# 105 idle matmuls of 256 and 512 columns behind the last product of a channel attention with an ELU feed-forward

## The chip, the cores and the metric

The kernel runs on one core of a Trainium2 chip. The metric is device time in microseconds (us). Before the change three runs took 2182.03, 2182.52 and 2183.09 us; the median, 2182.52 us, is the time before. One further execution was taken with the hardware profiler on. All views quoted below are of that execution, and its own time stands beside its span.

The engines are called by the profile's names: PE is TensorE's matmuls and PEld its weight loads, DVE is VectorE, ACT is ScalarE, POOL is GpSimd, SP is SyncE. L398 is line 398 of the kernel.

## The reference

Four batches of 6080 tokens with 256 channels. Attention is over channels: the Gram matrix of the normalised q and k is taken over all tokens of a batch, its softmax is applied to v, and the result goes through a feed-forward layer with ELU.

```python
B, N, C = (4, 6080, 256)
qn = q / (np.linalg.norm(q, axis=1, keepdims=True) + 1e-06)
kn = k / (np.linalg.norm(k, axis=1, keepdims=True) + 1e-06)
s = kn.transpose(0, 2, 1) @ qn / tau
a = softmax(s)                        # over the last axis
x = (v @ a).reshape(B * N, C)
h = x @ w_in                          # 256 -> 2048
g = np.where(h > 0, h, np.exp(np.minimum(h, 0)) - 1)
out = g @ w_out                       # 2048 -> 256
```

## The kernel before

**Tiles.** Tokens are cut into chunks of 512 or 496 columns (12 to a batch, 48 in all), the 2048 hidden channels into 16 blocks of 128 (`FT`), the 256 channels into two blocks of 128 (`KT`, `DT`). Per batch the attention matrix is multiplied into `w_in` first, and gives that batch's weights `wps[b]`. The main loop then runs over the steps (chunk, hidden block): six matmuls for the hidden block (`h_item`, L360 to L362), the ELU on ScalarE and VectorE (`elu`), a split of the result in a high and a low part (`split_g`, L107 and L108), and three steps later six matmuls into the chunk's two output banks (`out_item`, L398, L400, L402; one bank for each output half). Every wide matmul streams one chunk, 512 or 496 columns, through a weight tile of 128 columns. Each matmul has a weight load of its own, and the trace shows it as PEld.

**High and low parts.** Operands are float32 split into a part that one pass of TensorE takes and the rest. So three matmuls stand for one product. `in_turns` only sets in which order the columns of a chunk are streamed.

**Narrow matmuls before.** While a batch's main loop runs, the next batch's Gram matrix is made in between: `gram_item` gives a matmul of 512 columns (L191) and one of 256 (L198) in turn, and `out_item` takes one of them after each of its own. So a matmul of 256 columns always has one of 512 ahead of it and behind it. The norms of a batch (`norms`, L218) are eight float32 matmul passes of a single column each, in a row.

**The end.** For the last chunk `store` copies the first output half on ScalarE (L425), and the second half in two quarters of the output, one on VectorE (L419) and one on ScalarE (L420); each part is sent out as soon as it is copied (L427, L421, L422). Nothing else is left then.

**Order and buffers.** TensorE works in the order of its queue. PSUM has eight banks: two for the Gram matrices, three under the tag `w` (`WB = 3`: hidden blocks, attention, norms) and three under the tag `o` (`8 - KT - WB`: outputs). A tile that takes a bank waits for the last reader, and where there is none for the last writer, of the tile that had it three tiles before. `wo` holds `w_out` in its two parts for the whole run; `wps[3]` are the last batch's weights.

Of the kernel before, what the change touches and what calls it, by code (L numbers as in the profile page):

```python
# [7 lines left out]
F32 = mybir.dt.float32  # L8
# [19 lines left out]
def in_turns(cols):  # L28

    if len(cols.shape) == 3:  # L30
        return cols.rearrange("p x (a b) -> p x b a", a=2)
    return cols.rearrange("p (a b) -> p b a", a=2)
# [691 lines left out]
                fn()  # L724


# [1 line left out]
_INS = ["q", "k", "v", "tau", "moe_w_in", "moe_w_out"]  # L728
_OUTS = [((256, 24320), "float32")]
# [26 lines left out]
```

## Time and profile before

| what | value |
|---|---|
| runs before, us | 2182.03, 2182.52, 2183.09 |
| profiled execution, us | 2182.71 |
| its span in the trace, us | 2180.9 |
| matmuls in the trace | 10232 |
| matmuls of 256 columns at L198 | 276 |
| DMA | 118.15 MB, mean 54 GB/s |

The span is the time from the first to the last instruction of the trace; 1.81 us of the profiled execution lie around it. Busy time of an engine is the sum of its instructions' records. Matmul records overlap, since one begins while the one ahead is still draining, so their spacing from start to start is what a matmul costs in a stream. A timeline row has the start, the duration, the engine, the line, the operation, what is written from what, and the count; in brackets stands the idle time ahead of it and who ended that.

### The profile page before, as it was taken

Reading aid. Unit: us, or ns where it says so; the run is one execution under the profiler, and the core shown is the slowest. Engines: PE = TensorE matmul, PEld = TensorE weight load, DVE = VectorE, ACT = ScalarE, POOL = GpSimd, SP = SyncE. Lnnn points to the kernel's source line nnn. Section 1 sums busy time; section 2 is a strip of 40 time slices with the busy share of each in tenths; the row PEclk is TensorE's granted clock in tenths of the full one; section 3 lists DMA queues with packets and bytes.
Section 4 is the critical chain, followed back from the end, with each engine's and each line's share of the span. In section 5 each row is a group of like instructions: output and inputs, shape, how many; then the busy total and the mean of one; then the engine's idle time right before and its main releaser. Section 6 shows DMA issues by size and latency. Waiting matters only on the chain.

```text
span 2180.9 us, 27141 instructions
## 1 busy us (share of the span) xinstructions
PE 2169.1 (99%) x10232; PEld 1913.4 (88%) x10232; DVE 1519.3 (70%) x2395; ACT 1466.6 (67%) x2425; POOL 3.1 (0%) x11
## 2 busy tenths in 40 slices
PE   9999999999999999999999999999999999999999
PEld 7778888899888888889888888888988888888998
DVE  6996777777766777667776677677776666666665
ACT  5877766676767666666666666666666666666665
POOL 0000000000000000000000000000000000000000
PEclk9999999999999999999999999999999999999999
DMA  9220112111101111111020111121112000000000
GB/s 350 98 81 30 49 60 66 63 60 49 58 29 59 49 58 58 49 58 55 29 68 30 57 49 58 49 63 53 46 39 61 27 20 29 29 20 11 20 10 20
DMA packets 61092, 118.15 MB, mean 54 GB/s; under 512 B 6048, under 2 KB 15904, under 8 KB 60960
## 3 DMA queue, kind: packets, MB, share of 16 engines
q1 hardware_dynamic: 60816, 116.29, 16.3%
q8 instruction: 80, 1.31, 0.2%
q14 instruction: 52, 0.43, 0.1%
q10 hardware_dynamic: 144, 0.13, 0.0%
HBM read 89.39 MB, written 27.00 MB: 53 GB/s over the span
## 4 chain that ended last, share of the span: by engine, by line
PE 95%; DVE 2%; DMA 1%; ACT 1%; issue 0%; SPq 0%; DVEq 0%; ACTq 0%
PE po L398 15%; PE po L402 15%; PE po L400 15%; PE ph L360 15%; PE ph L362 15%; PE ph L361 15%; PE gram L191 3%; PE gram L198 1%; DVE acc L170 1%; DMA raw<-in_k_dram 1%; PE pw L319 0%; PE pw L320 0%; PE pw L318 0%; PE pw L315 0%; DMA room<-in_k_dram 0%
## 5 line engine op out<-in xcount | busy, mean ns | idle before, releaser
L107 ACT CAST g<-e 128x512 fp32r<-128x512 f32 (+1 forms) x768 | 470.7, 613 | 524.9 <-DVE e L377 285.7
L108 DVE TENSOR_TENSOR g<-e,g 128x512 fp32r<-128x512 f32 (+1 forms) x768 | 526.0, 685 | 346.0 <-ACT g L107 310.3
L398 PE MATMUL po<-g,wo 128*128 128x512 f32 (+1 forms) x1536 | 580.5, 378 | 2.5 <-DVE scr L415 2.1
L402 PE MATMUL po<-g,wo 128*128 128x512 f32 (+1 forms) x1536 | 579.5, 377 | 0.1
L400 PE MATMUL po<-g,wo 128*128 128x512 f32 (+1 forms) x1536 | 579.6, 377 | 0.0
L360 PE MATMUL ph<-vt,wp 128*128 128x512 f32 (+1 forms) x1472 | 557.1, 379 | 0.4 <-DVE e L373 0.4
L361 PE MATMUL ph<-vt,wp 128*128 128x512 f32 (+1 forms) x1472 | 555.0, 377 | 0.0
L362 PE MATMUL ph<-vt,wp 128*128 128x512 f32 (+1 forms) x1472 | 554.9, 377 | 0.0
L373 DVE SCALAR_TENSOR_TENSOR e<-e,ph 128x512 f32<-128x512 f32 (+1 forms) x416 | 283.5, 682 | 237.1 <-ACT e L372 237.1
L398 PEld LDWEIGHTS po<-g,wo 128*128 128x128 f32 x1536 | 290.8, 189 | 41.8 <-DVE scr L415 3.6
L400 PEld LDWEIGHTS po<-g,wo 128*128 128x128 f32 x1536 | 290.9, 189 | 37.1
L402 PEld LDWEIGHTS po<-g,wo 128*128 128x128 f32 x1536 | 291.2, 190 | 34.4 <-DVE g L108 0.5
L360 PEld LDWEIGHTS ph<-vt,wp 128*128 128x128 f32 x1472 | 278.6, 189 | 38.0 <-DVE e L373 1.0
L361 PEld LDWEIGHTS ph<-vt,wp 128*128 128x128 f32 x1472 | 278.7, 189 | 36.4 <-issue 0.7
L362 PEld LDWEIGHTS ph<-vt,wp 128*128 128x128 f32 x1472 | 278.7, 189 | 35.8 <-DVE wp L327 0.4
L371 ACT ACTIVATE e<-ph 128x512 f32<-128x512 f32 (+1 forms) x416 | 246.2, 592 | 94.5 <-PE ph L362 79.6
L372 ACT ACTIVATE e<-e 128x512 f32<-128x512 f32 (+1 forms) x416 | 261.2, 628 | 12.0
L377 DVE TENSOR_TENSOR e<-ph,e 128x512 f32<-128x512 f32 (+1 forms) x352 | 240.9, 684 | 10.6
L375 ACT ACTIVATE e<-ph 128x512 f32<-128x512 f32 (+1 forms) x352 | 207.8, 590 | 34.7 <-PE ph L362 32.2
L376 DVE TENSOR_SCALAR e<-e 128x512 f32<-128x512 f32 (+1 forms) x352 | 147.3, 418 | 21.8 <-ACT e L375 21.5
L170 DVE TENSOR_TENSOR acc<-acc,sq 128x1024 f32<-128x1024 f32 x84 | 102.5, 1221 | 14.3 <-ACT sq L169 13.6
L191 PE MATMUL gram<-qk 128*128 128x512 f32 x276 | 104.7, 379 | 0.0
(112 smaller groups left out, 1172.2 us busy)
## 6 DMA issues: line engine op xcount, KB each, us to landing
raw<-in_q_dram SPq DMA_DIRECT2D x73, 256.0 KB, 2.7
raw<-in_k_dram SPq DMA_DIRECT2D x73, 256.0 KB, 2.9
v<-in_v_dram SPq DMA_DIRECT2D x32, 512.0 KB, 3.7
out_dram<-o SPq DMA_DIRECT2D x56, 256.0 KB, 2.0
v<-in_v_dram SPq DMA_DIRECT2D x16, 496.0 KB, 3.6
out_dram<-o SPq DMA_DIRECT2D x31, 248.0 KB, 2.1
wraw<-w_scr SPq DMA_DIRECT2D x12, 512.0 KB, 3.3
room<-in_q_dram SPq DMA_DIRECT2D x16, 256.0 KB, 5.2
```

The costliest lines, as they stand in the source:

```text
L107: nc.scalar.copy(hi, src)
L108: nc.vector.tensor_sub(lo, src, hi.bitcast(F32))
L360: nc.tensor.matmul(ph[:, 0:n], wp[kt][:, 0, fs], hi, start=(kt == 0), stop=False)
L361: nc.tensor.matmul(ph[:, 0:n], wp[kt][:, 0, fs], lo, start=False, stop=False)
L362: nc.tensor.matmul(ph[:, 0:n], wp[kt][:, 1, fs], hi, start=False, stop=(kt == KT - 1))
L371: nc.scalar.activation(ev, pv, AF.Relu, scale=-1.0)
L372: x = nc.scalar.activation(ev, ev, AF.Exp, scale=-1.0)
L373: y = nc.vector.scalar_tensor_tensor(ev, ev, -1.0, pv, op0=ALU.add, op1=ALU.max)
L377: y = nc.vector.tensor_tensor(ev, pv, ev, op=ALU.max)
L398: nc.tensor.matmul(o, wo[:, f, 0, ds], hi, start=first(c, f), stop=False)
L400: nc.tensor.matmul(o, wo[:, f, 1, ds], hi, start=False, stop=False)
L402: nc.tensor.matmul(o, wo[:, f, 0, ds], lo, start=False, stop=last(c, f))
```

## The change

Behind the main loop, at the end of the kernel function, 105 matmuls are added. Their results go to PSUM tiles that nothing reads. They take their weights from the last batch's `wps` (the high part, 32 tiles of 128 columns) and stream columns of `wo`. There are three kinds: `W` streams 512 columns into a bank of the tag `o`; `N` streams 256 columns into half a bank of the tag `w`, three matmuls to a half and six to a tile; `n` is like `N`, but uses each weight tile twice in a row. They stand in this order: 24 N in a row; nine times N, W; nine times N, N, W; six times N, N, N, W; 12 n in a row.

```diff
+    flat = wo.rearrange("p f x d -> p (f x d)")
+    left = [wps[B - 1][kt][:, 0, x * P : x * P + P] for x in range(FT) for kt in range(KT)]
+    count = {"N": 0, "W": 0, "n": 0}
+    banks = {}
+
+    def idle(kinds):
+        for kind in kinds:
+            x = count[kind]
+            count[kind] += 1
+            if kind == "W":
+                bank = ps.tile([P, CH], F32, tag="o", bufs=8 - KT - WB, name="pw_idle")
+                nc.tensor.matmul(bank, left[x % 32], in_turns(flat[:, x % 8 * 2 * CH : x % 8 * 2 * CH + CH]), start=True, stop=True)
+                continue
+            y = x % 6
+            if y == 0:
+                banks[kind] = ps.tile([P, CH], F32, tag="w", bufs=WB, name="pn_idle")
+            w = left[(x if kind == "N" else x // 2) % 32]
+            o = banks[kind][:, y // 3 * 256 : y // 3 * 256 + 256]
+            m = in_turns(flat[:, x % 16 * CH : x % 16 * CH + 256])
+            nc.tensor.matmul(o, w, m, start=(y % 3 == 0), stop=(y % 3 == 2))
+
+    idle("N" * 24)
+    idle("NW" * 9)
+    idle("NNW" * 9)
+    idle("NNNW" * 6)
+    idle("n" * 12)
```

On TensorE the new rows stand behind the last product of the last chunk (`po_1` is its second output half, `wp_0` and `wp_1` the two channel blocks of the last batch's weights, `pn_idle` a narrow idle tile). A minus marks a row of before, a plus one of the change:

```order
 L400 MATMUL po_1_18006<-g,wo 128x496
 L402 MATMUL po_1_18006<-g,wo 128x496
-L751 UNCONDITIONAL_BRANCH
+L748 MATMUL pn_idle<-wo,wp_0_13714 128x256
+L748 MATMUL pn_idle<-wo,wp_1_13715 128x256
```

The program's closing branch moved behind the idle matmuls; ahead of them the queue is as it was.

The second place is on TensorE too, where the first wide ones come (`pw_idle`). The waits are on the signals of the engine named (`PE_49` is TensorE's own, `Activation_49` ScalarE's):

```order
+L748 MATMUL pn_idle<-wo,wp_0_13714 128x256 [waits PE_49]
+L740 MATMUL pw_idle<-wo,wp_0_13714 128x512
+L748 MATMUL pn_idle<-wo,wp_1_13715 128x256
+L740 MATMUL pw_idle<-wo,wp_1_13715 128x512 [waits Activation_49]
+L748 MATMUL pn_idle<-wo,wp_0_13714 128x256
+L740 MATMUL pw_idle<-wo,wp_0_13714 128x512 [waits Activation_49]
+L748 MATMUL pn_idle<-wo,wp_1_13715 128x256
+L740 MATMUL pw_idle<-wo,wp_1_13715 128x512 [waits PE_49]
```

The second and third wide ones wait for ScalarE's last two copies, which read the banks they take; from the fourth on they wait for TensorE itself, 24 such waits in all with three of the narrow kind, and 45 of the 105 give a signal.

## The prediction

> **What bounds the kernel now.** I read the page first (span, busy shares, granted clock, chain that ended last), then the end of the timeline, because the change adds work only behind the last product.
>
> ```profile
> span 2180.9 us, 27141 instructions
> ...
> PE 2169.1 (99%) x10232; PEld 1913.4 (88%) x10232; DVE 1519.3 (70%) x2395; ACT 1466.6 (67%) x2425; POOL 3.1 (0%) x11
> ...
> PEclk9999999999999999999999999999999999999999
> ...
> PE 95%; DVE 2%; DMA 1%; ACT 1%; issue 0%; SPq 0%; DVEq 0%; ACTq 0%
> ```
>
> TensorE is busy for 99% of the span and makes 95% of the chain, at full clock in all slices. So what is put in its queue costs time one for one, except where the program's end is set by something else. That is so only in the last microseconds. The next rows are the timeline there (start, duration, engine, line), and the time that the last output transfer takes.
>
> ```profile
> 2176.46 0.37 PE L398 MATMUL po<-g,wo 128*128 128x496 f32 x1
> ...
> 2176.66 0.57 ACT L425 COPY o<-po 128x496 f32<-128x496 f32 x1 [1.81 <-PE po L402]
> 2176.67 0.37 PE L400 MATMUL po<-g,wo 128*128 128x496 f32 x1
> ...
> 2176.88 0.37 PE L402 MATMUL po<-g,wo 128*128 128x496 f32 x1
> 2177.26 0.33 SPq L427 DMA_DIRECT2D out_dram<-o  x1
> 2177.29 0.42 DVE L419 COPY o<-po 128x248 f32<-128x248 f32 x1 [1.73 <-PE po L402]
> 2177.73 0.34 SPq L421 DMA_DIRECT2D out_dram<-o  x1
> 2177.74 0.36 ACT L420 COPY o<-po 128x248 f32<-128x248 f32 x1 [0.51 <-DVE o L419]
> 2178.13 0.37 ACTq L422 DMA_DIRECT2D out_dram<-o  x1
> ```
> ```profile
> out_dram<-o ACTq DMA_DIRECT2D x1, 124.0 KB, 1.9
> ```
>
> The last product starts at 2176.88 and its array would be free for another one 0.21 us later, at 2177.09, since matmuls of 496 columns start 0.21 us apart (2176.46, 2176.67, 2176.88) while each is recorded for 0.37 us. Behind it TensorE has nothing. The tail is copy, copy, transfer: the last transfer is issued at 2178.13 and lands 1.9 us later, at 2180.03. The span ends at 2180.9, so 0.87 us of closing follow. From 2177.09 to 2180.03 there are 2.94 us in which idle matmuls cost nothing. Past that, each of them moves the end.
>
> **The change part by part.** It removes and moves nothing: the other engines' rows stay as they were, and TensorE's stay up to the last product. It adds 105 matmuls: 24 + 9 + 18 + 18 + 12 = 81 narrow ones (256 columns) and 9 + 9 + 6 = 24 wide ones (512), each with a weight load of 128 columns. I need the spacing of each kind from start to start, not its recorded duration.
>
> Narrow matmuls among wide ones exist in this trace: the second product of a gram pair (L198).
>
> ```profile
> 300.29 0.38 PE L191 MATMUL gram<-qk 128*128 128x512 f32 x1
> 300.51 0.38 PE L400 MATMUL po<-g,wo 128*128 128x512 f32 x1
> 300.72 0.27 PE L198 MATMUL gram<-qk 128*128 128x256 f32 x1
> 300.83 0.38 PE L402 MATMUL po<-g,wo 128*128 128x512 f32 x1
> 301.05 0.38 PE L191 MATMUL gram<-qk 128*128 128x512 f32 x1
> 301.27 0.38 PE L398 MATMUL po<-g,wo 128*128 128x512 f32 x1
> ```
> ```profile
> 300.73 0.19 PEld L402 LDWEIGHTS po<-g,wo 128*128 128x128 f32 x1
> 300.83 0.19 PEld L191 LDWEIGHTS gram<-qk 128*128 128x128 f32 x1
> 301.05 0.19 PEld L398 LDWEIGHTS po<-g,wo 128*128 128x128 f32 x1
> ```
>
> Two wide ones take 300.72 - 300.29 = 0.43 us, so 0.216 each. The narrow one gives way after 0.11 us. The pair narrow plus wide takes 301.05 - 300.72 = 0.33 us. In the load rows, the load for L402 starts at 300.73, as soon as the narrow matmul runs, and the next load starts 0.10 us behind it: loads recorded for 0.19 us follow each other at nearly half that. So one narrow matmul between wide ones costs about 0.11 us.
>
> Narrow matmuls of this kind never stand in a row in this trace. Then every slot holds one weight load, and the load's own rhythm may be the bound. The nearest row is the norm sums (L218): eight loads in a row, each with a matmul of a single column, so that nothing but loads can set the pace.
>
> ```profile
> 1617.35 0.97 PEld L218 LDWEIGHTS pn<-ones,acc 128*128 128x128 f32 x8 [0.38 <-DVE acc L215]
> 1618.24 0.19 PEld L360 LDWEIGHTS ph<-vt,wp 128*128 128x128 f32 x1
> 1618.35 0.19 PEld L361 LDWEIGHTS ph<-vt,wp 128*128 128x128 f32 x1
> ```
>
> (0.97 - 0.19) / 7 = 0.111 us from load to load, and the two loads behind go on at 0.11. Streaming 256 columns takes 0.216 / 2 = 0.108 us. So loads and columns nearly balance, and loads bind by a hair. I take **0.112 us** for a narrow matmul in any place: above the 0.111 of the loads, under the 0.114 that the pair of 0.33 leaves beside 0.216. The low bound is 0.107 (the columns alone), the high bound 0.19 (loads that do not overlap at all, as their records are long). A wide one costs **0.216 us**. That the kind "n" uses each weight tile twice in a row brings nothing: L360 and L361 use the same tile in a row, and both have a load in the rows above.
>
> By stretch: 24 N 2.69; nine NW at 0.328, 2.95; nine NNW at 0.440, 3.96; six NNNW at 0.552, 3.31; 12 n 1.34. Sum **14.25 us** (81 x 0.112 + 24 x 0.216).
>
> A page of the Trainium skill weighs on this, "TensorE: Matmul & The Clock Gate". In "Back-to-back issue gap" it gives 262 cycles at 2.4 GHz for 256 columns and 518 for 512 (0.109 and 0.216 us), and in "LDWEIGHTS" 128 / 1.2 = 107 ns for a load; by these my estimate of the stretch would be 81 x 0.109 + 24 x 0.216 = 14.0 us. But the same section says that a real stream of load and matmul pairs runs at some 81 ns for 128 columns and 131 ns for 512. With 131 ns, the 24 wide ones would take 3.1 us in place of 5.2, and the end would come 2 us earlier. The rows above disagree: wide pairs here stand 0.216 us apart, and the measurement decides.
>
> Waits. The first wide idle one takes the third output bank, long free. The second and third take those of the last two products and wait for ScalarE's copies, which end at 2176.66 + 0.57 = 2177.23 and 2177.74 + 0.36 = 2178.10; they come up after 24 narrow ones, past 2179.8. No cost. From the fourth on, a wide one waits for TensorE itself, for the wide one three before it in the same bank: 21 waits, with three of the narrow kind for a tile that lies 13 matmuls or more back. A product counts as done 0.4 us after its start at most (ScalarE's L425 starts at 2176.66, before the product of 2176.67). The wide one three back began 3 x 0.328 - 0.112 = 0.87 us before the waiting load is due. So these waits are over by some 0.45 us when they are reached: 0. Behind a waiting matmul on TensorE stand only further idle ones, and no other engine waits for any of them. The banks, SBUF tiles and queues that they use serve nothing else any more.
>
> The end. The last idle one starts at 2177.09 + 14.25 - 0.11 = 2191.23 and is recorded for 0.27 us, as L198 is: 2191.50. The closing took 0.87 us behind the last landing, part of it SyncE waking up; I take 0.8. Span 2192.3 against 2180.9: **+11.4 us**. The profiled run took 2182.71 us (1.81 around its span, which stays), 0.19 above the median of 2182.52 of the three runs. 2182.52 + 11.4 = **2193.9 us**, 0.5% slower.
>
> **The rivals.**
>
> *Loads that exclude each other.* If back-to-back loads with full columns beside them took their recorded 0.19 us each, a narrow one would cost 0.19: 81 x 0.19 + 24 x 0.216 = 20.6 us, 6.3 more, 2200.2. For it speaks that no row shows narrow ones in a row, with loads and columns both at the limit; against it the 0.10 and 0.111 us above. Chance 0.07.
>
> *TensorE's waits for itself bite.* 45 of the idle matmuls signal and 24 wait for such a signal.
>
> ```profile
> PEld ph L360 <- PE po L402: 0.7, 3, 0.2
> ```
>
> This row (waits for TensorE's own products: us in total, times, longest) has 0.7 / 3 = 0.23 us for one that is not over yet. 24 x 0.23 = 5.5 us at most, 2199.4; it starts to decide where a signal comes more than 0.45 us later than reckoned. With half of that, 2196.6. Chance 0.07.
>
> *The clock drops.* It did so behind a pause of TensorE:
>
> ```profile
> 47.80:50.34 2.54, 0.01 (x1) 0.00 (x0) 2.35 (x3) 0.79 (x1) 0.00 (x0) 1.00 1.05 408
> ...
> 51.10:54.50 3.40, 3.40 (x10) 2.87 (x11) 2.04 (x10) 1.66 (x3) 0.00 (x0) 0.51 1.03 410
> 54.50:58.00 3.50, 3.50 (x18) 3.07 (x18) 2.73 (x8) 0.64 (x3) 0.00 (x0) 1.00 0.92 361
> ```
>
> (Columns: window, length, busy PE, PEld, DVE, ACT, POOL, granted clock, DMA share, GB/s.) After 2.5 us without work the clock stood at 0.51 for 3.4 us. One such spell would add 1.7 us, 2195.6. The idle stretch follows without a pause and streams columns in 0.108 of every 0.112 us. Chance 0.03.
>
> *Not slower: products that no one reads are not run.* If a later stage dropped them, or all but what fits in 2.94 us (26 narrow ones), the time would stay at 2182.5. But such work exists in the kernel before and stands in its trace:
>
> ```profile
> L210 PE MATMUL pd<-ones 128*128 128x128 f32 x8 | 2.1, 442 | 1.0 <-DVE ones L103 1.0
> ```
>
> These warming products are read by nothing. Chance 0.03.
>
> **How the numbers follow.** Forecast 2193.9, chance 0.80, in itself 2193.0 to 2194.9: 0.4 less with 0.107 for a narrow one, up to 0.5 by the runs' spread (2182.03 to 2183.09), and as much upward. The rivals have 0.07, 0.07, 0.03 and 0.03. For 8 in 10 with a margin the range takes in the clock spell and the milder waits: 2193.0 to 2196.6. A measurement of this kernel tells about 0.2% (4.4 us) from no change; all cases but the last are slower by more, so slower 0.97, same 0.02, faster 0.01 (something moved in the code ahead of the stretch).
>
> **What would show it.** In the profile after: span 2192.3, with the output copies and transfers at the same times as before; narrow matmuls 0.11 to 0.112 us apart in the first row of 24 (some 2.7 us in all), pairs NW at 0.33, NNW groups at 0.44, NNNW at 0.55; no idle time ahead of any idle matmul; the chain ending in TensorE at the new lines. Loads 0.19 us apart would be the first rival, gaps ahead of wide ones the second, a granted clock under 1 behind 2177 the third. The forecast is wrong if a row of narrow ones takes a rhythm that neither loads nor columns alone have here.

## The result, and the profile after

| | before | after |
|---|---|---|
| runs, us | 2182.03, 2182.52, 2183.09 | 2191.61, 2194.18, 2194.82 |
| median, us | 2182.52 | 2194.18 |
| profiled execution, us | 2182.71 | 2194.82 |
| its span, us | 2180.9 | 2193.0 |
| start of the last product to the end of the span, us | 2180.9 - 2176.88 = 4.02 | 2193.0 - 2177.57 = 15.43 |

The ratio is 1.0051, with a 95% interval of 1.0037 to 1.0065: 0.5% slower, as forecast (2193.9 us). The last row of the table leaves out everything ahead of the last product, and there the change costs 15.43 - 4.02 = **11.41 us**; 11.4 was forecast. The span is printed to 0.1 us; the expectations below use 4.05 and 15.48 for these two differences, from the unrounded trace, and the step between them is then 11.42 us.

From the page of the kernel after, the span, the busy shares and the granted clock:

```profile
span 2193.0 us, 27351 instructions
...
PE 2183.4 (100%) x10337; PEld 1928.2 (88%) x10337; DVE 1519.6 (69%) x2395; ACT 1466.4 (67%) x2425; POOL 3.1 (0%) x11
...
PEclk9999999999999999999999999999999999999999
```

10337 matmuls are 105 more than the 10232 of before: all of them run, though nothing reads their results. DVE and ACT keep their counts.

The timeline of all engines around the last product (start, duration, engine, line, what, count):

```profile
2177.35 0.57 ACT L425 COPY o<-po 128x496 f32<-128x496 f32 x1 [1.82 <-PE po L402]
...
2177.57 0.37 PE L402 MATMUL po<-g,wo 128*128 128x496 f32 x1
...
2177.94 0.33 SPq L427 DMA_DIRECT2D out_dram<-o  x1
2177.97 0.42 DVE L419 COPY o<-po 128x248 f32<-128x248 f32 x1 [1.73 <-PE po L402]
2178.42 0.33 SPq L421 DMA_DIRECT2D out_dram<-o  x1
2178.43 0.36 ACT L420 COPY o<-po 128x248 f32<-128x248 f32 x1 [0.51 <-DVE o L419]
2178.82 0.37 ACTq L422 DMA_DIRECT2D out_dram<-o  x1
```

The copies and transfers come as before, in the same distances: the last one is issued 1.25 us behind the start of the last product, as it was. Only everything stands 0.69 us later (2177.57 against 2176.88); that comes from the start of the kernel, see the fifth experiment. The timeline of TensorE alone behind it:

```profile
2177.77 2.95 PE L748 MATMUL pn_idle<-wo,wp 128*128 128x256 f32 x25
2180.56 0.38 PE L740 MATMUL pw_idle<-wo,wp 128*128 128x512 f32 x1
2180.78 0.27 PE L748 MATMUL pn_idle<-wo,wp 128*128 128x256 f32 x1
2180.89 0.38 PE L740 MATMUL pw_idle<-wo,wp 128*128 128x512 f32 x1
...
2183.40 0.38 PE L748 MATMUL pn_idle<-wo,wp 128*128 128x256 f32 x2
2183.62 0.38 PE L740 MATMUL pw_idle<-wo,wp 128*128 128x512 f32 x1
2183.84 0.39 PE L748 MATMUL pn_idle<-wo,wp 128*128 128x256 f32 x2
...
2190.11 0.50 PE L748 MATMUL pn_idle<-wo,wp 128*128 128x256 f32 x3
2190.44 0.38 PE L740 MATMUL pw_idle<-wo,wp 128*128 128x512 f32 x1
2190.66 1.50 PE L748 MATMUL pn_idle<-wo,wp 128*128 128x256 f32 x12
```

25 narrow ones (24 and the first of the pairs) fill 2177.77 to 2180.56: 2.79 / 25 = 0.112 us each. A pair NW takes 2180.89 - 2180.56 = 0.33, an NNW group 2183.84 - 2183.40 = 0.44, an NNNW group 2190.66 - 2190.11 = 0.55. The last record ends at 2190.66 + 1.50 = 2192.16, and the closing takes 0.84 us more.

The clock row of the page can't show a short spell: a slice is 55 us long, and a 9 stands for 90% or more. A window view over the idle stretch can (window, length, busy time of five engines, granted clock, DMA share, GB/s); the granted clock is 1.00:

```profile
2177.00:2193.00 16.00, 15.16 (x110) 14.26 (x108) 0.42 (x1) 0.94 (x2) 0.00 (x0) 1.00 0.09 33
```

The groups of the two new lines, with the idle time ahead of them as the last figure:

```profile
L748 PE MATMUL pn_idle<-wo,wp 128*128 128x256 f32 x81 | 13.1, 275 | 0.0
...
L740 PE MATMUL pw_idle<-wo,wp 128*128 128x512 f32 x24 | 8.7, 382 | 0.0
```

No idle time stands ahead of any. That alone rules no wait out, since a narrow record of 0.275 us reaches over the next two starts; experiment 4 has waits that are felt, and hardly any idle time. The spacing decides: from the first wide one to the row of 12 stand 24 wide and 44 narrow ones, for which 24 x 0.216 + 44 x 0.112 = 10.11 us was reckoned without any wait, and it is 2190.66 - 2180.56 = 10.10. All 21 waits of wide ones lie in there, so none was felt.

### The profile page after: what moved, and what is told of

Its sections match the earlier page's. It is cut to its first block, busy times and chain, and to the rows that moved or that the text cites. A ratio compares the mean times of both kernels' runs of the same rounds, so it can differ in the third digit from the quotient of the medians.

```text
span 2193.0 us, 27351 instructions
## 1 busy us (share of the span) xinstructions
PE 2183.4 (100%) x10337; PEld 1928.2 (88%) x10337; DVE 1519.6 (69%) x2395; ACT 1466.4 (67%) x2425; POOL 3.1 (0%) x11
## 4 chain that ended last, share of the span: by engine, by line
PE 95%; DVE 2%; ACT 1%; DMA 1%; issue 0%; SPq 0%; DVEq 0%; ACTq 0%
PE po L398 15%; PE po L400 15%; PE po L402 15%; PE ph L360 15%; PE ph L362 15%; PE ph L361 15%; PE gram L191 3%; PE gram L198 1%; DVE acc L170 1%; DMA raw<-in_k_dram 1%; PE pw L318 0%; PE pw L320 0%; PE pw L319 0%; PE pw L315 0%; PE pn_idle L748 0%
## 5 line engine op out<-in xcount | busy, mean ns | idle before, releaser
L402 PE MATMUL po<-g,wo 128*128 128x512 f32 (+1 forms) x1536 | 579.8, 378 | 0.1
L360 PE MATMUL ph<-vt,wp 128*128 128x512 f32 (+1 forms) x1472 | 557.5, 379 | 0.4 <-DVE e L373 0.4
L402 PEld LDWEIGHTS po<-g,wo 128*128 128x128 f32 x1536 | 291.3, 190 | 34.3 <-DVE g L108 0.5
L360 PEld LDWEIGHTS ph<-vt,wp 128*128 128x128 f32 x1472 | 278.8, 189 | 38.0 <-DVE e L373 1.0
```

The lines of the kernel that those rows point to most:

```text
L360: nc.tensor.matmul(ph[:, 0:n], wp[kt][:, 0, fs], hi, start=(kt == 0), stop=False)
L402: nc.tensor.matmul(o, wo[:, f, 0, ds], lo, start=False, stop=last(c, f))
```

## The experiments

Unless said otherwise a kernel here is the changed one, with other idle matmuls at the same place.

**1. What the end of the kernel covers.** Only the first row is kept.

```diff
     idle("N" * 24)
-    idle("NW" * 9)
-    idle("NNW" * 9)
-    idle("NNNW" * 6)
-    idle("n" * 12)
```

> Only the first row of 24 narrow matmuls is kept behind the last product. My theory: the copies and the last transfer cover the first 2.94 us behind the last product, and 24 x 0.112 = 2.69 us fit in; from the start of the last product to the end of the span it stays at the 4.05 us of before (2176.88 to 2180.9), and the time at 2182.5 us (within 0.1%). Rival, every added matmul costs from the first on: 2.7 us more, 6.7 us from the last product to the end and 2185.2 us in all.

Measured: 2182.29 us, 2182.15 for the kernel before on the same chip; ratio 1.0002 (0.9993 to 1.0011). The timeline of this kernel:

```profile
2174.83 0.37 PE L402 MATMUL po<-g,wo 128*128 128x496 f32 x1
...
2175.04 2.84 PE L748 MATMUL pn_idle<-wo,wp 128*128 128x256 f32 x24
...
2176.09 0.37 ACTq L422 DMA_DIRECT2D out_dram<-o  x1
```

The idle row ends at 2175.04 + 2.84 = 2177.88. The transfer issued at 2176.09 takes 1.9 us, to 2177.99. So the row is over just ahead of the landing, and from 2174.83 to the span's end at 2178.9 it is 4.07 us, against 4.02 before. The cover is real: 24 matmuls cost nothing that can be measured. The rival's 2.7 us (0.12%) lie just outside the interval, which ends at 0.11%.

**2. What sets the pace of narrow matmuls in a row.** Other widths, and weight tiles of half the columns.

```diff
+    def row(cols, weights=P, many=12):
...
+            nc.tensor.matmul(bank[0:weights, 0:cols], left[x % 32][:, 0:weights], m, start=(x % 3 == 0), stop=(x % 3 == 2))
+    for cols in (64, 128, 192, 224, 256, 272, 288, 320, 384):
+        row(cols)
+    row(128, 64)
+    row(256, 64)
```

> In place of the 105 stand eleven rows of 12 matmuls: 64, 128, 192, 224, 256, 272, 288, 320 and 384 columns with weight tiles of 128 columns, then 128 and 256 columns with weight tiles of 64 columns. My theory, weight loads of 128 columns set the pace up to the width where streaming takes longer: 0.112 us from start to start for 64 to 256 columns alike, then the columns: 0.115 for 272 or a little more, 0.122 for 288, 0.135 for 320, 0.162 for 384. With half the weight columns the load takes half: 0.056 us at 128 columns (there columns and loads are level) and 0.108 to 0.109 at 256. Rival, the columns set the pace (load hidden): 0.027 at 64, 0.054 at 128, 0.081 at 192, 0.108 at 256, and no difference with narrower weight tiles. Rival, a fixed cost per matmul: 0.112 up to 256 whatever the weight tile's width.

It was profiled once (2191.68 us). Rows of its timeline from inside eight of the eleven stretches of 12 (the span from the first's start to the last's end, and the count; 128\*64 is a weight tile of 64 columns):

```profile
2173.85 1.06 PE L737 MATMUL pn_idle<-wo,wp 128*128 128x64 f32 x8
...
2175.22 1.06 PE L737 MATMUL pn_idle<-wo,wp 128*128 128x128 f32 x8
...
2179.40 1.06 PE L737 MATMUL pn_idle<-wo,wp 128*128 128x256 f32 x8
...
2180.52 1.09 PE L737 MATMUL pn_idle<-wo,wp 128*128 128x272 f32 x8
...
2182.04 1.14 PE L737 MATMUL pn_idle<-wo,wp 128*128 128x288 f32 x8
...
2185.22 1.46 PE L737 MATMUL pn_idle<-wo,wp 128*128 128x384 f32 x8
...
2186.90 0.63 PE L737 MATMUL pn_idle<-wo,wp 128*64 128x128 f32 x8
...
2187.77 1.04 PE L737 MATMUL pn_idle<-wo,wp 128*64 128x256 f32 x8
```

and the groups that give the duration of one record:

```profile
L737 PE MATMUL pn_idle<-wo,wp 128*128 128x384 f32 x12 | 2.1, 326 | 0.0
...
L737 PE MATMUL pn_idle<-wo,wp 128*128 128x288 f32 x12 | 1.6, 286 | 0.0
...
L737 PE MATMUL pn_idle<-wo,wp 128*128 128x256 f32 x12 | 1.5, 276 | 0.0
L737 PE MATMUL pn_idle<-wo,wp 128*64 128x256 f32 x12 | 1.5, 273 | 0.0
...
L737 PE MATMUL pn_idle<-wo,wp 128*64 128x128 f32 x12 | 0.9, 222 | 0.0
```

A row of eight lasts seven spacings and one record. At 256 columns (1.06 - 0.276) / 7 = 0.112 us, and the rows of 128 and 64 columns are just as long: a quarter of the columns saves nothing. At 288 columns (1.14 - 0.286) / 7 = 0.122, at 384 (1.46 - 0.326) / 7 = 0.162: there the columns set the pace, at 0.42 ns each. With weight tiles of 64 columns, 128 columns cost (0.63 - 0.222) / 7 = 0.058 and 256 cost (1.04 - 0.273) / 7 = 0.110. So the loads set the pace up to some 260 columns, and 256 stand just under the point where the two are level. A narrower weight tile also gives half as many rows of results, and no run separates that from the load; that the pace is the load's is supported by the norm sums of the prediction, with 0.111 us at a single column. Both rivals fall: columns alone would have given 0.027 us at 64, and a fixed cost would not have fallen with the narrower tile.

All of this is for the split operands (the kernel's `F32R` tiles). The kernel before also has matmuls of 256 columns in a row on operands that are not split (`F32` tiles, L484):

```profile
59.07 1.89 PE L484 MATMUL pe<-scr 128*128 128x256 f32 x8
```

A record there is 0.379 us long, so (1.89 - 0.379) / 7 = 0.216 us from start to start, twice as much for the same width.

**3. The same 105 where nothing covers them.** The stretch is issued behind the store of chunk 40 and not at the end; `idle` is as in the change, but stands ahead of the main loop.

```diff
                 store(c, f, pos.pop(c))
+                if c == 40:
+                    left += [wps[B - 1][kt][:, 0, x * P : x * P + P] for x in range(FT) for kt in range(KT)]
+                    idle("N" * 24 + "NW" * 9 + "NNW" * 9 + "NNNW" * 6 + "n" * 12)
```

> The same 105 idle matmuls, but behind the products of chunk 40, with seven chunks of real work still to come, none at the end. My theory: TensorE is the bound there and nothing covers them, so they cost their whole stretch, 14.2 us: 2182.5 + 14.2 = 2196.7 us, that is 2.9 us more than at the end (by the same start of the kernel). From the last product to the end of the span 4.05 us as before. Rival, the other engines catch up in the meantime and what they cost TensorE later comes back: less than 14.2 us, towards 11. Rival, the idle stretch starves the loop behind it: over 14.5 us.

Measured: 2197.54 us against 2182.15, ratio 1.0071 (1.0059 to 1.0084), that is 12.9 to 18.3 us. The runs of before spread by some 5 us, in part for a reason that the fifth experiment shows: the granted clock. Its mean is 0.998 in four of the five runs here but in only six of the 15 beside them, so the 15.4 us between the medians are too many. The trace decides. TensorE's timeline where the stretch begins and where the loop goes on (the first row is of the first eight idle ones):

```profile
1895.68 1.05 PE L718 MATMUL pn_idle<-wo,wp 128*128 128x256 f32 x8
...
1909.90 0.38 PE L360 MATMUL ph<-vt,wp 128*128 128x512 f32 x1
1910.12 0.38 PE L361 MATMUL ph<-vt,wp 128*128 128x512 f32 x1
...
2190.77 0.37 PE L402 MATMUL po<-g,wo 128*128 128x496 f32 x1
```

The stretch takes 1909.90 - 1895.68 = 14.22 us, and the loop goes on at its usual 0.22 us behind it. From the first L360 to the last L402 it is 2127.12 us (63.65 to 2190.77), before 2112.82 (64.06 to 2176.88): 14.30 more. The end takes 2194.8 - 2190.77 = 4.03 us, as before. So nothing is absorbed and nothing starved: the stretch costs its full length here, and 2.8 us less at the end.

**4. When a wait of TensorE for itself is felt.** Every matmul takes a bank of its own, from six, three or two banks in turn; this takes the place of the 105, and was profiled once (2194.66 us).

```diff
+    def row(cols, tags, many=18):
+        for x in range(many):
+            tag = tags[x % len(tags)]
+            bank = ps.tile([P, CH], F32, tag=tag, bufs={"w": WB, "o": 8 - KT - WB, "gram": KT}[tag], name="pn_idle")
...
+    row(256, ["w", "o"])
+    row(256, ["w"])
+    row(256, ["gram"])
+    row(512, ["w"])
+    row(512, ["gram"])
```

> In place of the 105 stand five rows of 18 matmuls in which every one takes a bank of its own and waits for TensorE's own earlier product in that bank: 256 columns six banks deep, three deep, two deep; then 512 columns three deep and two deep. My theory: such a wait costs nothing as long as it reaches back further than the time until a product counts as done (some 0.31 us behind the start for 256 columns, 0.41 for 512) plus a load's 0.11. So 0.112 us from start to start six deep; three deep it bites: (0.31 + 0.11) / 3 = 0.14; two deep 0.21; 512 columns three deep 0.216, no cost, two deep (0.41 + 0.11) / 2 = 0.26. Rival, a satisfied wait costs by itself: over 0.112 six deep too. Rival, a wait drains the array: about 0.4 and more at every depth.

Loads from inside each of the five rows, in that order (PEld; a load's own record is 0.19 us):

```profile
2175.27 1.20 PEld L737 LDWEIGHTS pn_idle<-wo,wp 128*128 128x128 f32 x10
...
2177.71 1.49 PEld L737 LDWEIGHTS pn_idle<-wo,wp 128*128 128x128 f32 x10
...
2180.33 2.36 PEld L737 LDWEIGHTS pn_idle<-wo,wp 128*128 128x128 f32 x11
...
2183.82 2.78 PEld L737 LDWEIGHTS pn_idle<-wo,wp 128*128 128x128 f32 x13
...
2188.24 2.90 PEld L737 LDWEIGHTS pn_idle<-wo,wp 128*128 128x128 f32 x11
```

Six banks: (1.20 - 0.19) / 9 = 0.112 us. Three: (1.49 - 0.19) / 9 = 0.144, as a mean. Two: (2.36 - 0.19) / 10 = 0.217. With 512 columns three banks (2.78 - 0.19) / 12 = 0.216, two (2.90 - 0.19) / 10 = 0.271. Forecast were 0.112, 0.14, 0.21, 0.216 and 0.26. Two banks give back the delay itself: 2 x 0.217 - 0.11 = 0.32 us from a narrow one's start until the wait for it is over, 2 x 0.271 - 0.11 = 0.43 for a wide one. A satisfied wait costs nothing, and an unsatisfied one costs just what is missing; no drain comes on top. Three banks fit the same delay: (0.32 + 0.11) / 3 = 0.143.

Almost none of this stands in the view of waits, since overlapping records hide it. Its only row for these 90 matmuls is (us in total, times, longest):

```profile
PEld pn_idle L737 <- PE pn_idle L737: 0.2, 1, 0.2
```

**5. Why the runs differ by microseconds.** The kernel before, without any idle stretch, has the ten warming matmuls of this edit in the pause in which TensorE waits for the first batch's norms.

```diff
+        keep_warm(10)
         pn, dg, rk, nm, ready = norms(0, acc)
```

> The kernel before, without the idle stretch, but with ten warming matmuls (ones by ones, 128 columns, float32, 20 passes of some 0.11 us, 2.2 us in all) in TensorE's pause of 1.3 to 2.8 us ahead of the first batch's norms near 47 us. My theory: the runs differ by whether the granted clock falls to half behind that pause, for none, 3.4 or 6.8 us (mean granted clock 1.0, 0.999, 0.998); a filled pause leaves none. So clock 1.0 in all runs, a spread of under 2 us, and a median like that of the runs of before with clock 1.0: 2179 to 2181 us, 1 to 3 us under before. Rival, the clock falls for another reason: the same three clocks and 2182 us. Rival, the filling makes the norms late: 2183 us or more.

Measured: median 2180.3 us over 11 runs (2179.29 to 2183.53), 2181.58 for the kernel before; ratio 0.9993 (0.9984 to 1.0002). Nine of the 11 runs have a mean granted clock of 1.0 and two 0.999; of the 15 runs of before beside them, one has 1.0, eight 0.999 and six 0.998. A window view shows the stretch right behind the pause (window, length, busy time of five engines, granted clock, DMA share, GB/s). The kernel before:

```profile
50.00:57.00 7.00, 6.65 (x27) 5.81 (x28) 4.07 (x16) 1.66 (x3) 0.00 (x0) 0.76 1.04 413
```

The kernel after, in the same window:

```profile
50.00:57.00 7.00, 7.00 (x20) 5.78 (x21) 3.15 (x13) 1.66 (x3) 0.00 (x0) 0.52 0.83 328
```

And this kernel:

```profile
50.00:57.00 7.00, 6.86 (x37) 5.76 (x37) 5.21 (x19) 2.75 (x7) 0.00 (x0) 1.00 0.93 365
```

The clock is at half for about 3.4 us in the first, 6.8 us in the second and not at all in the third. What that costs stands between the norms (L218) and the first step of the main loop (L360). TensorE's timeline before:

```profile
50.35 1.28 PE L218 MATMUL pn<-ones,acc 128*128 128x1 f32 x8 [2.53 <-DVE acc L215]
...
64.06 0.57 PE L360 MATMUL ph<-vt,wp 128*128 128x512 f32 x1
```

and after:

```profile
49.38 1.47 PE L218 MATMUL pn<-ones,acc 128*128 128x1 f32 x8 [2.55 <-DVE acc L215]
...
64.78 0.57 PE L360 MATMUL ph<-vt,wp 128*128 128x512 f32 x1
```

That is 13.71 us before and 15.40 after; with the pause filled it is 12.46 (49.63 to 62.09). So the shorter spell costs 1.25 us and the longer one 2.94. The 0.69 us by which the last product came later after the change are two things: 1.69 us more for the longer spell, and 0.97 less because the norms began earlier in that execution. The norms begin anywhere from 48.1 to 50.4 us in the ten traces, and why was not tested.

So the clock accounts for a part of the runs' spread, and the start of the norms for another. The spread of under 2 us was a miss: the two runs with 0.999 took 2181.82 and 2183.53, and the nine with 1.0 alone lie between 2179.29 and 2182.11.

**6. A stretch that is half covered.** 48 narrow ones in place of the 105, profiled once (2185.29 us).

```diff
-    idle("N" * 24)
-    idle("NW" * 9)
-    idle("NNW" * 9)
-    idle("NNNW" * 6)
-    idle("n" * 12)
+    idle("N" * 48)
```

> 48 narrow matmuls in place of the 105. My theory: 48 x 0.1117 = 5.36 us, of which 2.9 lie beside the last copies and transfer, less 0.1 as the closing starts behind the drained array; from the start of the last product to the end of the span 0.21 + 5.36 - 0.11 + 0.28 + 0.88 = 6.62 us, against 4.05 before. Rival, a fixed cost as soon as TensorE ends last: more than 7.2 us.

The last product starts at 2176.91, the span ends at 2183.5: 6.59 us, where 6.62 was expected.

```profile
2176.91 0.37 PE L402 MATMUL po<-g,wo 128*128 128x496 f32 x1
2177.11 5.52 PE L748 MATMUL pn_idle<-wo,wp 128*128 128x256 f32 x48
```

So past the cover the cost grows with the stretch, with no step where TensorE becomes the last one.

**7. Both together.** The changed kernel with the ten warming matmuls of experiment 5.

> The changed kernel with its 105 idle matmuls, and the ten warming matmuls in the pause as well. My theory: both effects add: 15.48 us from the last product to the end as in the changed kernel, granted clock 1.0 until then, a median of 2179 to 2181 plus 11.4, 2190.4 to 2192.4 us, with a spread under 2 us. Rival, the clock falls for another reason: 2193.6 us.

Measured: 2191.38 us (2190.78 to 2192.28, five runs), all at clock 1.0; 15.5 us from the last product (2174.38) to the end of the span (2189.9). Both effects add, and in these five runs without a spell of half clock the spread is 1.5 us.

**8. A longer filling.** 16 warming matmuls in the kernel before.

```diff
+        keep_warm(16)
         pn, dg, rk, nm, ready = norms(0, acc)
```

> As the warmed kernel without the idle stretch, with 16 warming matmuls (some 3.5 us) in place of ten, after which 1.1 us of the pause were still left and two of eleven runs still had a mean clock of 0.999. My theory, the clock falls only behind a pause that is long enough: clock 1.0 in all runs and a spread under 2 us, but some 1.2 us of warming that is too long for the pause may go on TensorE's path: median 2179.5 to 2181.5. Rival, those two had another reason: some runs with 0.999 as before.

Measured: 2180.7 us (2180.31 to 2182.82), 2181.5 for the kernel before; ratio 0.9995 (0.9986 to 1.0004). All 11 runs have clock 1.0, against three of the 15 beside them. All but one lie within 1.1 us, the last 1.4 above these. So the spread is 2.5 us where under 2 was expected, a second miss, and this time with the full clock in every run. Neither this filling nor that with ten is faster than the kernel before beyond its interval; the medians are 0.8 and 1.3 us lower.

## Why the prediction was right

- **The path.** That TensorE's queue sets the time, and only the last microseconds are free, held: the same stretch costs 14.3 us in the middle, 11.4 at the end, and its first 24 matmuls nothing.
- **The spacing.** 0.112 us for a narrow one and 0.216 for a wide one gave 14.25 us; measured were 14.22 by the middle stretch. The reading that loads and columns nearly balance at 256 columns, with loads ahead by a hair, is shown by the widths: the pace does not move from 64 to 256 columns, and halves with the weight tile. No run shows the low bound of 0.107: where the columns alone set the pace, 256 cost 0.110.
- **A row that was overlooked.** The section on the kernel before says that a matmul of 256 columns always has one of 512 ahead of it and behind it. That holds for L198, but not for the rows of L484 (experiment 2), where 256 columns cost 0.216 us. By this nearest row in width the 81 narrow ones would have cost 8.4 us more. The idle ones stream split operands, as L198 does, and went at 0.112; the prediction took the right rows (L198 and L218), but did not name this one as a rival.
- **The weights used twice** brought nothing: the last row of 12 has the pace of the others, (1.50 - 0.28) / 11 = 0.111 us.
- **The waits.** Forecast at nothing, with 0.45 us to spare. The spacing of the groups shows none (10.10 us for 10.11), and experiment 4 gives the price where the reach is too short. The delay until a product counts as done is 0.43 us for a wide one, a little more than the 0.4 "at most" of the working; the reach of 0.87 us left room for that.
- **The closing** was sized at 0.8 us, and took 0.84 by the page. That a part of the 0.87 us before is SyncE waking up is not shown by any run: the closing is about as long behind TensorE's last record as behind the last landing.
- **The start** was left out of the sum. The span came out at 2193.0 and not 2192.3: in the profiled execution after, the spell of half clock at 50 us was longer (1.69 us), and the norms began 0.97 us earlier. That the median of three, 2194.18, lies 0.3 us from the forecast is luck in part: 2191.61 to 2194.82 is a wider band than the 0.5 us either way that was allowed for. The 11.41 us of the trace do not rest on that luck.
- **The rivals.** Loads that exclude each other fall by experiment 2, the waits by the spacing of the groups and experiment 4, products that are not run by the count of 10337. The clock did not fall in the stretch (1.00 in the window view), but it did at the place from which that rival's price was read; a spell of 3.4 us, priced at 1.7 us, cost 1.25 there. "At full clock in all slices" was more than the tenths of the page can say, since this spell lies in one of them.

## What to carry to other kernels

A short matmul costs the larger of its columns and its weight load; here the two meet at some 260 columns for split operands and weight tiles of 128 columns (operands that are not split took 0.216 us for 256 columns), so splitting below that buys nothing unless the weight tile shrinks as well. Read the cost of a matmul from start to start and not from its record, and ask of added work at the end how long the last copies and transfers cover it. A bank that TensorE takes again from itself cost nothing here where its last product had begun 3 x 0.216 = 0.65 us earlier (512 columns, three banks), and two banks, 0.43 us, were too few; by the delay of experiment 4 the limit is near 0.43 + 0.11 = 0.54 us, an estimate.

## What had not been expected of the hardware

The kernel's own runs fall into three groups by one event, though the groups overlap, since each spreads by 2 to 3 us in itself. Over the 45 runs of before that were taken beside experiments 1 to 4, 5 to 7 and 8, the mean granted clock was 1.0 in eight (median 2179.9 us), 0.999 in 20 (2181.3) and 0.998 in 17 (2183.3). In the traces that is a spell at half clock behind a pause of TensorE of only 1.9 to 2.8 us, which lasts 3.41 us or 6.83 us by the clock's own records, or does not come.

The Trainium skill, in "TensorE: Matmul & The Clock Gate", section "Part 1: The HAM clock gate (the "warmup" mystery)", describes a free-running window of 3413 ns over which the activity is judged, with half rate behind an idle one. Both lengths fit whole windows of that size. But here half rate came behind pauses shorter than a window (2.5 us before, and 1.9 us in the first experiment's trace, where it is 2.8 with the norms' single-column matmuls behind it), and in the fourth experiment's run a pause of 2.6 us brought none; the measurement decides. What sets the length of a spell stays open: 2.5 us of pause stand ahead of one of 3.41 before, and of one of 6.83 after.
